# Masks in two float32r parts, a place of its own for one tile's values, and the head's order: one edit to an attention and expert kernel

## The chip, the cores and the metric

One Trainium2 chip, one core. The metric is the device time of one execution in microseconds (us); three executions of the kernel before gave 692.93, 693.51 and 694.43, so the median is 693.51.

## The reference

The reference is an attention followed by a gated feed-forward layer. For 4 batches of 8 heads, 768 positions and 64 dimensions, each query sees the keys within 15 positions of its own, and besides them 24 summary keys, one for each block of 32 positions (the maximum of the block's keys, with log 32 added to their scores). The softmax runs over both together, and the values are the positions' own and the blocks' means:

```python
k_sum = k.reshape(B, H, nb, block, D).max(axis=3)
v_sum = v.reshape(B, H, nb, block, D).mean(axis=3)
scores_l_m = np.where(mask_l, scores_l, -1000000000.0)
scores_all = np.concatenate([scores_l_m, scores_s], axis=-1)
...
return np.matmul(a, v_all).astype(np.float32)
```

Its result, 3072 rows of 512, goes through `(x @ w_a * (x @ w_b)) @ w_out` with 1536 hidden columns.

## The kernel before

**Units.** A tile is 128 query rows, and a unit (`u`) is two tiles, so 24 tiles make 12 units. The hidden columns are cut into 12 slices `f` of 128. The pair (unit, slice) is an item: `hidden` (L977) makes 24 float32r matmuls of 256 columns for both products, ScalarE and VectorE multiply them and split the result in two parts (`gh`, `gl`), and `down` (L996) adds six float32r matmuls of 512 columns into two banks. The 144 items are nearly all of TensorE's work. Their order is (0,0), (0,1), (1,0), (0,2), (1,1), (0,3) and so on, then units 2 to 11 one after the other (L1023).

**Weights.** The weights reach the kernel as 64-bit numbers, in 36 parts of 512 KB (w_a, w_b and w_out of each slice), two parts to a pair `j` (0 to 17), so slice f uses parts 3f, 3f+1 and 3f+2. `convert(j)` (L290) turns a pair into two float32r parts: for each half a ScalarE pass (L313) and three VectorE passes (L321, L328, L334), then a ScalarE copy (`hi`, L366) and two GpSimd passes (L371, L377, the second writes `lo`). The last three run over the whole pair at once, or, where `single` holds, over one half at a time. For pairs 0 and 1 and the last four `single` holds.

**The first two units** (tiles 0 to 3, L768 to L883) have a softmax of their own: `masks` (L590) writes the mask into two banks by a float32 matmul against the identity, the scores (L604) are added to it, VectorE takes the maxima (L637), ScalarE the exponentials (L649), VectorE makes a diagonal of the reciprocal sums (L671), TensorE turns and scales by it (L692), ScalarE copies the result (L704), and `values` (L755, matmuls L737) multiplies with the tile's values. The result is split into `x` (L745, L748), and a unit's items need the `x` of both its tiles. `begin(g)` (L825) makes query turn, masks and scores of tile g, `end(g)` (L838) the rest. Values lie in `vbuf` for tiles 0 and 2 and in `vw1` for tiles 1 and 3, so the load for tile 2 waits for the product of tile 0. The block means of the values are made once (L848 to L871) and copied by GpSimd from `vbuf` to `vw1` (L874).

**Order.** Every operation is given to `work.add` with an engine, a rank, an estimated duration and the names it reads and writes; `emit` (L72) is a list scheduler that writes the program out, engine by engine, by estimated times. The table `ORDER` (L23) shifts, for the operation of a given number, its rank and gives it an estimated time before which it isn't placed. These times exist in the planning only; on the chip each engine runs its instructions in the order written. SP issues all loads in one queue. Unit 2's attention (`FILL`) is spread among the conversions; its tile's GpSimd passes are L679.

Of the kernel before, what the change touches and what calls it, by code (L numbers as in the profile page):

```python
# [20 lines left out]


ORDER = {  # L23
# [15 lines left out]
}  # L39


# [65 lines left out]
def attention_moe(  # L107
# [10 lines left out]
    nc = tc.nc  # L118
# [96 lines left out]


    spaces = {n: sb([P, 2048], n) for n in ("S0", "S1")}
    for j in (*range(8, 13), *range(NW - 3, NW)):
        spaces[f"W{j}"] = wp.tile([P, 2048], F32, tag=f"W{j}", name=f"space{j}")

    pown = spaces["S0"][:, 2 * CV :].rearrange("p (h c x) -> p h c x", h=2, x=P)
# [5 lines left out]
    def spot(i):  # L227
        n, x = f"W{8 + i // 2}", i % 2 * 2
        return spaces[n][:, x * 512 : (x + 2) * 512], (f"{n}.{x}", f"{n}.{x + 1}")


    work = Work({"POOL": 10.0, "DVE": 4.0, "ACT": 3.0, "PE": 4.0, "SP": 0.8})
# [57 lines left out]
    def convert(j):  # L290
        rank = CONVERT + j / 6
        rk = [f"raw{2 * j}", f"raw{2 * j + 1}"]

        if j < NW - 4:
            space = {12: "W16", 13: "W17"}.get(j, ("W17", "W16", "W15", "S0")[j % 4])
            places = [(space, 0, 2), (space, 1, 3)]
            single = j < 2
        else:
            places = [slots[(2 * (j - NW + 4) + h) % 3] for h in range(2)]
            places = [(n, x, x + 1) for n, x in places]  # L300
            single = True
        cols = [[slice(x * CV, (x + 1) * CV) for x in xs] for _, *xs in places]
        fx, px = [[spaces[places[h][0]][:, cols[h][x]] for h in range(2)] for x in range(2)]
        fk, pk = [[f"{places[h][0]}.{places[h][1 + x]}" for h in range(2)] for x in range(2)]
        spans = [(h,) for h in range(2)] if single else [(0, 1)]

        def scale(h):
            high = raws[j][:, 2 * h * CV : 2 * (h + 1) * CV].rearrange("p (n t) -> p n t", t=2)
            nc.scalar.activation(  # L313
                bank["c0"], high[:, :, 1].bitcast(F32), AF.Prelu, scale=2.0**-112, alpha=-(2.0**32)
            )


        def step(n, h):
            f, p, e, s = fx[h], px[h], bank["c0"], bank["c1"]
            if n == 0:  # L320
                nc.vector.tensor_scalar(  # L321
                    out=f.bitcast(I32), in0=e.bitcast(I32), scalar1=3, scalar2=None,
                    op0=ALU.logical_shift_left,
                )
            elif n == 1:


                nc.vector.tensor_scalar(  # L328
                    out=s.bitcast(I32), in0=f.bitcast(I32), scalar1=-(1 << 23), scalar2=None,
                    op0=ALU.bitwise_and,  # L330
                )
            else:
                low = raws[j].rearrange("p (n t) -> p n t", t=2)[:, h * CV : (h + 1) * CV, 0]
                nc.vector.scalar_tensor_tensor(  # L334
                    out=p, in0=low.bitcast(U32), scalar=2.0**-52, in1=s, op0=ALU.mult, op1=ALU.mult
                )

        for n, h in [(n, h) for h in range(2) for n in range(3)]:
            f, p, e, s, r = [fk[h]], [pk[h]], ["c0"], ["c1"], [rk[h]]
            if n == 0:  # L340
                act(CHAIN, 0.52, r, e, lambda h=h: scale(h))
            reads, writes = ((e, f), (f, s), (r + s, p + [f"done{j}"] + r))[n]
            dve(rank, 0.6, reads, writes, lambda n=n, h=h: step(n, h))

        def parted(part):
            if j not in homes:
                homes[j] = wp.tile([P, 8, 2, P], F32R, tag=f"W{j}", name=f"w{j}")
            return homes[j][:, :, part, :]

        for hs in spans:  # L350
            ms = slice(4 * hs[0], 4 * (hs[-1] + 1))
            f, p, hi, lo = (
                [x[h] for h in hs] for x in (
                    fk, pk, [f"hi{2 * j}", f"hi{2 * j + 1}"], [f"lo{2 * j}", f"lo{2 * j + 1}"]
                )
            )
            x0 = spaces[places[hs[0]][0]]
            f8, p8 = (
                x0[:, cols[hs[0]][x].start : cols[hs[-1]][x].stop].rearrange(
                    "p (m n) -> p m n", n=P  # L360
                )
                for x in range(2)
            )
            act(
                rank - 0.5, 0.25 + 0.37 * len(hs), f + rk, hi,
                lambda ms=ms, f8=f8: nc.scalar.copy(out=parted(0)[:, ms], in_=f8),  # L366
            )
            takes = 0.2 + 1.1 * len(hs)
            pool(
                rank + 0.1 * hs[0], takes, hi, f,  # L370
                lambda ms=ms, f8=f8: nc.gpsimd.tensor_tensor(  # L371
                    out=f8, in0=f8, in1=parted(0)[:, ms].bitcast(F32), op=ALU.subtract
                ),
            )
            pool(
                rank + 0.1 * hs[0], takes, f + p, lo,
                lambda ms=ms, f8=f8, p8=p8: nc.gpsimd.tensor_tensor(  # L377
                    out=parted(1)[:, ms], in0=f8, in1=p8, op=ALU.add
                ),
            )  # L380
# [201 lines left out]
    def scores(u, t, qT, qk, s, sk, banks, diag=None, lead=None):  # L582
# [6 lines left out]

        def masks():  # L590
            for h in range(2):
                nc.tensor.matmul(
                    bank[banks[h]].rearrange("p (c x) -> p c x", x=P), ident,
                    mask[:, kind, None, :].broadcast_to([P, NP, P]), start=True, stop=False,
                )

        def fn():
            for c in range(NP):
# [10 lines left out]
                        )  # L609

        if masked:
            pe(rank + 0.1, 1.8, [], banks, masks)
        if lead is None:
            pe(-1, 1.2, [qk] + KT, banks, fn)
        else:
# [151 lines left out]

    def first_attention():  # L768
        first_keys()
        q0, qk = spot(3)  # L770
        for t in range(2):
            load(
# [25 lines left out]
        k0, k1 = key  # L798
        vk1 = [k0, k1, k1 + "b", k0 + "s", k1 + "s"]

        vin = []
        for i in range(6):
            x, key = spot(4 + i // 2)
# [4 lines left out]
            vin.append((x, key))  # L808
        load_values(0, 0, vbuf, VK[:3], 16)
        load_values(0, 1, vw1, vk1[:3], 18)  # L810

        q1, qk1 = spot(1)
        for t in range(2):
# [24 lines left out]
        def end(g, bk):  # L838
            u, i = g // G, g % G
            transposes(u, g, s[i], sk[i], [f"o{2 * i}", f"o{2 * i + 1}"], pts[i])  # L840
            values(u, g, (vbuf, vw1)[i], (VK, vk1)[i], bk, pts[i])

        for t in range(2):
            begin(t, f"h{t}")
# [19 lines left out]
        for e, r0 in ((0, WIN), (1, 32)):  # L864
            rows = slice(r0, r0 + 32)
            act(
                FIRST, 0.6, ["h0"], [VK[3 + e]],
                lambda e=e, rows=rows: nc.scalar.copy(
                    out=vbuf[e][rows].rearrange("p h d -> p (h d)"), in_=bank["h0"][rows]
                ),  # L870
            )  # L871
            pool(
                FIRST, 0.8, [VK[3 + e]], [vk1[3 + e]],
                lambda e=e, rows=rows: nc.gpsimd.tensor_copy(out=vw1[e][rows], in_=vbuf[e][rows]),  # L874
            )
        end(0, "h1")
        load_values(0, 2, vbuf, VK[:3], 20.5)
        begin(2, "o0")
        end(1, "h0")
        load_values(0, 3, vw1, vk1[:3], 20.7)  # L880
        begin(3, "o2")
        end(2, "o0")
        end(3, "o2")  # L883
# [196 lines left out]
```

## Time and profile before

| | us |
|---|---|
| median of three executions | 693.51 |
| the profiled execution | 693.23 |
| its span from the first to the last instruction | 691.5 |
| TensorE busy in the span | 676.8 |
| VectorE, ScalarE, GpSimd busy | 433.4, 252.7, 186.2 |

The profiled execution is 1.73 us longer than its span (start and end of the program), and 0.28 us below the median. The profile names the engines PE (TensorE), PEld (its weight load), ACT (ScalarE), DVE (VectorE), POOL (GpSimd) and SP (SyncE, here the queue of the loads). A float32 matmul shows as two records, a float32r one as one. An idle time in brackets says what ended it.

### The profile page before, as it was taken

Reading aid. Unit: us, or ns where it says so; the run is one execution under the profiler, and the core shown is the slowest. Engines: PE = TensorE matmul, PEld = TensorE weight load, DVE = VectorE, ACT = ScalarE, POOL = GpSimd, SP = SyncE. Lnnn points to the kernel's source line nnn. Section 1 sums busy time; section 2 is a strip of 40 time slices with the busy share of each in tenths; the row PEclk is TensorE's granted clock in tenths of the full one; section 3 lists DMA queues with packets and bytes.
Section 4 is the critical chain, followed back from the end, with each engine's and each line's share of the span. In section 5 each row is a group of like instructions: output and inputs, shape, how many; then the busy total and the mean of one; then the engine's idle time right before and its main releaser. Section 6 shows DMA issues by size and latency. Waiting matters only on the chain.

```text
span 691.5 us, 15093 instructions
## 1 busy us (share of the span) xinstructions
PE 676.8 (98%) x5988; PEld 621.5 (90%) x5988; DVE 433.4 (63%) x988; ACT 252.7 (37%) x795; POOL 186.2 (27%) x226
## 2 busy tenths in 40 slices
PE   6799999999999999999999999999999999999997
PEld 4589999998999999999999999999999999999996
DVE  3899999986676668766764767653662762212221
ACT  4886565523323333134333232332332332211211
POOL 5669899732433210412110110110110110000000
PEclk9999999999999999999999999999999999999999
DMA  9999863465144126431212311300200100000000
GB/s 229 260 276 225 267 163 121 81 134 111 49 103 104 40 40 124 96 72 42 53 24 60 67 29 46 67 1 22 66 22 2 54 22 1 31 1 1 32 1 31
DMA packets 154943, 54.84 MB, mean 79 GB/s; under 512 B 132456, under 2 KB 147816, under 8 KB 154872
## 3 DMA queue, kind: packets, MB, share of 16 engines
q1 hardware_dynamic: 154872, 53.88, 33.4%
q8 instruction: 47, 0.77, 0.5%
q14 instruction: 24, 0.20, 0.1%
HBM read 47.12 MB, written 6.29 MB: 77 GB/s over the span
## 4 chain that ended last, share of the span: by engine, by line
PE 93%; DMA 2%; SPq 2%; DVE 1%; ACT 1%; issue 0%; POOL 0%; ACTq 0%
PE h L965 57%; PE o L1001 29%; PE o L737 2%; PE c L737 2%; SPq L249 2%; PE c L604 2%; PE o L604 1%; DMA raw<-in_moe_w_out_dram 1%; DMA space<-in_v_dram 1%; PE o L692 1%; SPq L278 0%; DVE nml L637 0%; ACT s L649 0%; DVE pt L671 0%; ACT c L313 0%
## 5 line engine op out<-in xcount | busy, mean ns | idle before, releaser
L965 PEld LDWEIGHTS h<-x,w 128*128 128x128 f32 x3456 | 413.1, 188 | 10.5 <-issue 0.2
L965 PE MATMUL h<-x,w 128*128 128x256 f32 x3456 | 415.4, 277 | 0.0
L985 DVE TENSOR_TENSOR h<-h,g 128x256 f32<-128x256 f32 x144 | 62.0, 431 | 165.2 <-ACT g L982 163.4
L1001 PE MATMUL o<-w,gh 128*128 128x512 f32 x576 | 157.6, 396 | 0.0
L982 ACT COPY g<-h 128x256 f32<-128x256 f32 x144 | 53.6, 372 | 282.3 <-PE h L965 281.5
L1001 PEld LDWEIGHTS o<-w,gh 128*128 128x128 f32 x576 | 99.0, 188 | 17.2 <-ACT x L745 1.5
L679 POOL TENSOR_TENSOR s<-s,nml 128x512 f32<-128x512 f32 x40 | 41.6, 1041 | 242.6 <-DVE nml L664 242.1
L723 DVE STREAM_TRANSPOSE pt<-s 32x256 f32<-32x256 f32 x228 | 99.4, 436 | 5.6 <-POOL s L679 1.5
L1001 PE MATMUL o<-w,gl 128*128 128x512 f32 x288 | 90.2, 394 | 0.0
L990 DVE TENSOR_TENSOR gl<-h,gh 128x256 fp32r<-128x256 f32 x144 | 60.6, 421 | 30.9 <-ACT gh L987 29.4
L649 ACT ACTIVATE s<-s,nml 128x128 f32<-128x128 f32 x160 | 62.3, 392 | 43.9 <-DVE nml L637 43.9
L987 ACT CAST gh<-h 128x256 fp32r<-128x256 f32 x144 | 53.4, 371 | 60.7 <-DVE h L985 60.2
L1001 PEld LDWEIGHTS o<-w,gl 128*128 128x128 f32 x288 | 53.7, 188 | 11.8 <-issue 0.3
L534 POOL TENSOR_TENSOR S<-S 96x64 f32<-96x64 f32 (+3 forms) x54 | 35.5, 657 | 40.5 <-DMA S<-in_v_dram 29.5
L649 ACT ACTIVATION_READ_ACCUMULATOR s<-s,nml 128x1 f32 x160 | 30.1, 188 | 0.0
L371 POOL TENSOR_TENSOR space<-space,w 128x1024 f32<-128x1024 f32 (+1 forms) x13 | 26.8, 2063 | 6.0 <-ACT w L366 5.8
L658 DVE TENSOR_SCALAR nml<-nml 128x4 f32<-128x4 f32 x40 | 9.5, 239 | 28.6 <-ACT s L649 28.6
L313 ACT ACTIVATE c<-raw 128x512 f32<-128x512 f32 x36 | 23.3, 647 | 11.2 <-DVE space L321 4.1
L377 POOL TENSOR_TENSOR w<-space 128x1024 fp32r<-128x1024 f32 (+1 forms) x13 | 26.8, 2059 | 1.0
L637 DVE TENSOR_REDUCE nml<-s 128x4 f32<-128x512 f32 x40 | 25.3, 666 | 0.0
L433 POOL COPY kT<-ksum 128x144 f32<-128x144 f32 x16 | 4.7, 306 | 66.7 <-DVE ksum L511 52.0
L371 POOL TENSOR_TENSOR S<-S,w 128x512 f32<-128x512 f32 (+1 forms) x11 | 17.5, 1595 | 6.8 <-ACT w L366 6.8
(104 smaller groups left out, 457.3 us busy)
## 6 DMA issues: line engine op xcount, KB each, us to landing
raw<-in_moe_w_a_dram SPq DMA_DIRECT2D x12, 512.0 KB
raw<-in_moe_w_b_dram SPq DMA_DIRECT2D x12, 512.0 KB
raw<-in_moe_w_out_dram SPq DMA_DIRECT2D x12, 512.0 KB
out_dram<-S SPq DMA_DIRECT2D x24, 256.0 KB
qin<-in_q_dram SPq DMA_DIRECT2D x160, 32.0 KB
S<-in_v_dram SPq DMA_DIRECT2D x24, 192.0 KB
vw<-in_v_dram SPq DMA_DIRECT2D x18, 192.0 KB
kin<-in_k_dram SPq DMA_DIRECT2D x24, 100.0 KB
```

What stands on the lines that cost most here:

```text
L371: lambda ms=ms, f8=f8: nc.gpsimd.tensor_tensor(out=f8, in0=f8, in1=parted(0)[:, ms].bitcast(F32), op=ALU.subtract),
L534: lambda: nc.gpsimd.tensor_tensor(out=out, in0=i0, in1=i1, op=ALU.add),
L649: lambda h=h, c=c, sums=sums: nc.scalar.activation(s[h][:, c, :], x[h][:, c, :], AF.Exp, bias=m[:, 0, h, c : c + 1], scale=1.0, accum_out= ...
L679: lambda h=h, r=r: nc.gpsimd.tensor_tensor(out=s[h], in0=s[h], in1=r[:, :, None].broadcast_to([P, NP, P]), op=ALU.mult,),
L723: lambda js=js, qs=qs: nc.vector.transpose(out=pv[js, :, qs], in_=sv[qs, :, js]),
L737: nc.tensor.matmul(ps[h * D : (h + 1) * D, c, es], vw[e][:, 2 * c + h, :], d[:, h, c, es], start=True, stop=True, tile_position=(0, h * D),)
L965: nc.tensor.matmul(ps, w[:, c, part, :], x[xpart][:, c, :], start=(i == 0), stop=(i == n - 1))
L982: act(CHAIN, 0.38, [hk], [gk], lambda: nc.scalar.copy(out=g, in_=pa))
L985: lambda: nc.vector.tensor_tensor(out=pa, in0=pb, in1=g, op=ALU.mult),
L987: act(CHAIN, 0.41, [hk], [ghk], lambda: nc.scalar.copy(out=gh, in_=pa))
L990: lambda: nc.vector.tensor_tensor(out=gl, in0=pa, in1=gh.bitcast(F32), op=ALU.subtract),
L1001: nc.tensor.matmul(bank[ok[j]], (gh if first else gl)[:, js], w[:, :, part, :], start=(f == 0 and first and part == 0), stop=(f == NF - 1 ...
```

## The change

Four edits. (1) GpSimd makes a float32r copy of the identity and of two of the three masks, as a rounded part and a remainder, and `masks` adds both parts with float32r matmuls (estimate 0.96 in place of 1.8). (2) Tile 2's values get a place `vw2`, are loaded with those of tiles 0 and 1, and GpSimd copies the block means there too; tile 3 loads into `vbuf`. (3) `convert` takes the pair j = 2 half by half. (4) The table `ORDER` is replaced by another; as operations come and go, the numbers stand for others than before. Cut to its core:

```diff
-    136: (0, 41.8), 139: (38.79, 0), 141: (-0.3, 32.8), 142: (-3.38, 36.5), 149: (7.63, 29.8),
...
+    54: (31.73, 15.8), 55: (-2.09, 15.8), 56: (1.09, 14.9), 69: (30, 20.8), 76: (3.37, 22.1),
...
+    141: (-0.15, 41), 143: (19.54, 37.9), 144: (29.29, 0), 147: (-7.99, 32.8), 148: (0, 34.2),
...
+    235: (0, 46.4), 236: (-69.66, 47.4), 240: (47.6, 14), 241: (6.98, 14), 242: (-5.91, 42.5),
...
+    356: (1.15, 79.1), 405: (-40.68, 88.5), 412: (29.12, 89.5), 420: (19.57, 0),
...
-    for j in (*range(8, 13), *range(NW - 3, NW)):
+    for j in (*range(8, 14), *range(NW - 3, NW)):
...
+    x, MK = spot(10)
+    x = x.bitcast(F32R)
+    identr = x[:, :P]
+    maskr = [
+        x[:, n : n + 2 * P].rearrange("p (i x) -> p i x", x=P) for n in (P, 4 * P)
+    ]
...
-            single = j < 2
+            single = j < 3
...
-                nc.tensor.matmul(
-                    bank[banks[h]].rearrange("p (c x) -> p c x", x=P), ident,
-                    mask[:, kind, None, :].broadcast_to([P, NP, P]), start=True, stop=False,
-                )
+                for part in range(2):
+                    nc.tensor.matmul(
+                        bank[banks[h]].rearrange("p (c x) -> p c x", x=P), identr,
+                        maskr[part][:, kind, None, :].broadcast_to([P, NP, P]),
+                        start=(part == 0), stop=False,
+                    )
...
-            pe(rank + 0.1, 1.8, [], banks, masks)
+            pe(rank + 0.1, 0.96, MK, banks, masks)
...
+        for takes, fn in (
+            (0.3, lambda: nc.gpsimd.tensor_copy(out=identr, in_=ident)),
+            (0.45, lambda: nc.gpsimd.tensor_copy(out=maskr[0], in_=mask[:, :2, :])),
+            (0.6, lambda: nc.gpsimd.tensor_tensor(
+                out=maskr[1], in0=mask[:, :2, :], in1=maskr[0].bitcast(F32), op=ALU.subtract
+            )),
+        ):
+            pool(-1, takes, [], MK, fn)
...
+        x, (k0, k1) = spot(2)
+        vw2 = [x[:, e * 512 : (e + 1) * 512].rearrange("p (h d) -> p h d", d=D) for e in range(2)]
+        vk2 = [k0, k1, k1 + "b", k0 + "s", k1 + "s"]
+        work.add("-", 0, 0, 0, (), vk2, lambda: None)
...
+        load_values(0, 2, vw2, vk2[:3], 18.5)
...
-            values(u, g, (vbuf, vw1)[i], (VK, vk1)[i], bk, pts[i])
+            values(u, g, (vbuf, vw1, vw2, vbuf)[g], (VK, vk1, vk2, VK)[g], bk, pts[i])
...
+            for dst, dk in ((vw1, vk1), (vw2, vk2)):
...
-        load_values(0, 2, vbuf, VK[:3], 20.5)
...
-        load_values(0, 3, vw1, vk1[:3], 20.7)
+        load_values(0, 3, vbuf, VK[:3], 20.7)
```

## Rows read from the trace of the kernel before

**Rows 1.** The page: TensorE's total; VectorE's busy tenths in 40 slices of 17.3 us

```profile
PE 676.8 (98%) x5988; PEld 621.5 (90%) x5988; DVE 433.4 (63%) x988; ACT 252.7 (37%) x795; POOL 186.2 (27%) x226
...
DVE  3899999986676668766764767653662762212221
```

**Rows 2.** Chain that ended last, 0 to 140 us: start, duration, what

```profile
24.75 8.94 DMA raw<-in_moe_w_out_dram
...
33.77 0.64 ACT c L313
...
45.94 2.92 PE h L965 x24
...
72.77 1.37 PE o L1001 x6
```

**Rows 3.** TensorE in order of time, 0 to 120 us: start, duration, instructions

```profile
30.06 1.98 PE L592 MATMUL o<-mask,ident 128*128 128x512 f32 x4 [0.32 <-ACT qT L832]
...
34.97 1.98 PE L592 MATMUL o<-mask,ident 128*128 128x512 f32 x4 [1.45 <-ACT space L832]
36.88 1.15 PE L737 MATMUL h<-space,space 128*64 128x64 f32 x32
...
39.97 3.00 PE L965 MATMUL h<-x,w 128*128 128x256 f32 x24
...
44.79 1.15 PE L737 MATMUL o<-pt,vw 128*64 128x64 f32 x30 [0.59 <-ACT pt L704]
45.87 2.99 PE L965 MATMUL h<-x,w 128*128 128x256 f32 x24
...
54.59 5.61 PE L965 MATMUL h<-x,w 128*128 128x256 f32 x48
...
63.03 5.62 PE L965 MATMUL h<-x,w 128*128 128x256 f32 x48
...
99.93 2.91 PE L965 MATMUL h<-x,w 128*128 128x256 f32 x24
```

**Rows 4.** ScalarE and SP in order of time, around 34 us

```profile
34.34 0.58 ACT L832 ACTIVATE space<-o 128x512 f32<-128x512 f32 x1
...
34.18 3.65 SPq L249 DMA_DIRECT2D vw<-in_v_dram  x3
```

**Rows 5.** Mask matmuls (L592) by stretch: length, PE and PEld busy, granted clock, DMA share, GB/s

```profile
5.20:8.60 3.40, 3.33 (x4) 1.08 (x4) 1.00 1.31 223
...
12.00:14.00 2.00, 1.86 (x4) 0.55 (x4) 1.00 1.08 347
```

**Rows 6.** All engines by stretch: length, PE, PEld, DVE, ACT, POOL busy, clock, DMA, GB/s

```profile
20.00:30.00 10.00, 7.85 (x75) 6.33 (x74) 8.37 (x18) 9.61 (x34) 4.39 (x7) 1.00 1.17 264
30.00:40.00 10.00, 8.49 (x117) 5.59 (x117) 8.88 (x18) 8.38 (x27) 8.70 (x7) 1.00 1.15 292
```

**Rows 7.** GpSimd in order of time, 27 to 100 us

```profile
27.19 1.27 POOL L874 COPY space<-vw 32x512 f32<-32x512 f32 x2 [4.37 <-ACT vw L868]
28.55 1.28 POOL L371 TENSOR_TENSOR space<-space,w 128x512 f32<-128x512 f32 x1
...
43.15 2.36 POOL L377 TENSOR_TENSOR w<-space 128x1024 fp32r<-128x1024 f32 x1
49.31 2.38 POOL L371 TENSOR_TENSOR S<-S,w 128x1024 f32<-128x1024 f32 x1 [3.80 <-ACT w L366]
51.77 2.40 POOL L377 TENSOR_TENSOR w<-S 128x1024 fp32r<-128x1024 f32 x1
54.82 2.43 POOL L371 TENSOR_TENSOR space<-space,w 128x1024 f32<-128x1024 f32 x1 [0.65 <-ACT w L366]
...
62.34 2.42 POOL L377 TENSOR_TENSOR w<-space 128x1024 fp32r<-128x1024 f32 x1
...
92.33 1.04 POOL L679 TENSOR_TENSOR s<-s,nml 128x512 f32<-128x512 f32 x1
...
97.24 2.42 POOL L377 TENSOR_TENSOR w<-S 128x1024 fp32r<-128x1024 f32 x1
```

More of the change, by code (lines that the diff above doesn't have):

```diff
@@ L229, in spot @@
         return spaces[n][:, x * 512 : (x + 2) * 512], (f"{n}.{x}", f"{n}.{x + 1}")
+    x, MK = spot(10)
[4 more added lines that the diff above has]
+    ]
+    MK = list(MK)
     work = Work({"POOL": 10.0, "DVE": 4.0, "ACT": 3.0, "PE": 4.0, "SP": 0.8})
@@ L871, in first_attention @@
             )
[L872 to L875, printed above, removed]
+            for dst, dk in ((vw1, vk1), (vw2, vk2)):
+                pool(
+                    FIRST, 0.8, [VK[3 + e]], [dk[3 + e]],
+                    lambda e=e, rows=rows, dst=dst: nc.gpsimd.tensor_copy(
+                        out=dst[e][rows], in_=vbuf[e][rows]
+                    ),
+                )
         end(0, "h1")
-        load_values(0, 2, vbuf, VK[:3], 20.5)
         begin(2, "o0")
         end(1, "h0")
-        load_values(0, 3, vw1, vk1[:3], 20.7)
+        load_values(0, 3, vbuf, VK[:3], 20.7)
         begin(3, "o2")
```

28 rows, old and new, of the table ORDER are left out of this document.

## The prediction, made before the changed kernel was run

> **What bounds the kernel now.** I read the page first: TensorE is busy for 676.8 of 691.5 us [rows 1], so there are under 15 us in which it stands still, and a tuning of the head can win no more than a part of these plus whatever TensorE work it removes. Next the chain that ended last, from its early end: up to about 45 us it runs over loads, ScalarE and VectorE, and from 45.94 us on over TensorE alone [rows 2]. So the time is the moment at which TensorE starts to run without gaps, plus a fixed amount of matmul work behind it. Then TensorE's own order of time [rows 3]: the first item starts at 39.97, the second at 45.87, and between 30 and 46 us it idles three times: 0.32 us, 1.45 us and 0.59 us. The long one, ahead of 34.97, is tile 3's mask waiting for its query turn to be read by ScalarE (34.34 to 34.92 [rows 4]), and that reading stands in ScalarE's queue behind a conversion that waited for weights landing at 33.69 [rows 2]. Tile 1's product, ready to run, is behind that mask and starts at 36.88; on it hangs the `x` of unit 0 and so the first item.
>
> What could hold TensorE back after that is the supply of weights. VectorE is at nine tenths or more from the second to the eighth slice [rows 1], and it idles only 1.63 + 1.12 = 2.75 us between 20 and 40 us [rows 6]. GpSimd writes the last part of a pair, and how late that is shows the slack: pair 3 ends at 51.77 + 2.40 = 54.17, item (0,2) starts at 54.59; pair 5 ends at 64.76, item (0,3), the second half of the block at 63.03, starts at 65.8; pair 11 ends at 99.66, item (0,7) starts at 99.93 [rows 3, 7]. The slack is 0.4, 1.0 and 0.3 us. A gain in the head stays a gain only if these three move too.
>
> **The change part by part.**
>
> Masks. A tile's masks are two float32 matmuls in four records: 1.91 us from 34.97 to the next start at 36.88 [rows 3]. Six float32r matmuls of the same 512 columns take 1.37 us in steady flow [rows 2], 0.23 each, so the four new ones take 0.92. That is 1.0 us less for each of four tiles. Tiles 0 and 1 stand in a stretch where TensorE waits for loads, so I count nothing there: the cover is the loads, and without it each would give its 1.0. Tiles 2 and 3 stand at 30.06 and 34.97 on the path to the first items, and I count 0.95 each, 1.9 together.
>
> GpSimd's three preparing passes (a 128x128 copy, a 128x256 copy, a 128x256 subtraction) have no row of their own; from below they cost nothing beside the loads, from above one two-input 128x512 pass each (1.28 us [rows 7]), 3.8 us. They stand before the first score, in a stretch in which GpSimd has only the mask's making behind it. I take nothing on the path. The two more copies of the block means are 0.64 us each like the two at 27.19, 1.3 us; these start after a wait of 4.37 us [rows 7], and if they are late they push pair 0 behind them by 1.3. Pairs 0 to 2 can bear that: with it and ten half passes of 1.3 each behind 28.55, pair 2's first half is ready at 42.9, before the second item's place. So I take nothing and keep 1.3 for the range.
>
> Tile 2's values. The load moves from 34.18 [rows 4] to the loads of tiles 0 and 1. It was not the wait: tile 2's product at 44.79 waited for ScalarE's copy of the turned scores [rows 3]. By itself this part is worth nothing. It costs three issues in SP's queue and (96 + 32 + 64) rows of 2 KB, 384 KB, at 264 GB/s [rows 6] 1.5 us, ahead of weights that land at 33.69. Those are pair 2's second half, whose copy the new table holds to 47.4 planned us, so the cover is that later use; if it is gone, the pair is 1.5 us late. Tile 3's load into `vbuf` waits for tile 0's product as tile 2's did.
>
> Pair 2 by halves. Item (0,1) needs the first half only (part 4). Before, both halves end together at 43.15 + 2.36 = 45.51 [rows 7], just ahead of the item at 45.87 [rows 3], so without this part nothing won earlier could start the second item earlier. Two half passes of 1.28 us let the first half be ready about 2.5 us sooner; the price is 4 x 1.28 = 5.1 us for 4.8.
>
> The order. Counting the operations through, the new table places tile 1's product (now 148) from 34.2 planned us, before from 36.5, and no longer behind tile 3's masks. I therefore count the 1.45 us of TensorE's wait as won. It holds the first half of pair 2 to 46.4 and the second to 47.4, which says that they go behind other work in their queues; the first query turn of unit 2 goes to 79.1 planned us, so its softmax passes, two of 1.04 us at 92.33 ahead of pair 11 [rows 7], go later.
>
> The sum. 1.9 + 1.45 = 3.35 us are won before the second item. How much of it lasts is set by supply: at (0,7) 0.3 of slack plus the 2.1 of the two passes that move behind pair 11, 2.4; at (0,3) 1.0 plus the 2.75 that VectorE idles early, 3.75. The smallest is 2.4 us. The profiled execution's 693.23 becomes 690.8; the median stands 0.28 above it, so I forecast 691.1. Bounds: below, all three waits between 30 and 46 us (2.36) and both masks (1.9) are won and supply refuses nothing, 4.3 us, so 689.2, and a part of tile 0's and 1's masks may come on top; above, nothing is won and the 1.3 of the copies reaches the path, 694.8.
>
> **The rivals.**
>
> The supply binds at once. VectorE has no work less than before, and the conversions decide at 54.17, 64.76 and 99.66 [rows 7]. If its new order brings pairs 3 to 5 no earlier, TensorE only waits later, and the gain is the slack, 0.3 us: 693.2. For it: the holds of pairs 3 and 8 in the new table lie within a microsecond or two of the old planned places. Against it: (1,0) can run before (0,2) once unit 1 is ready, which gives pair 3 another 2.75 us.
>
> The clock. The four records of tile 0's mask take 3.33 us of busy time in 5.2 to 8.6 us and another tile's 1.86 in 12 to 14 [rows 5], so TensorE ran there at about half rate (the lower of 1.2 and 2.4 GHz), though the row's granted clock reads 1.00, and full rate came after this dense work. Now the masks wait for GpSimd, and the early stretch holds only turns between loads. If the low rate lasts until the masks of tiles 0 and 1 are done, these cost 2 x 0.92 more, 1.8 us, and the gain shrinks to 0.6: 692.9. The Trainium skill, "TensorE: Matmul & The Clock Gate", section "What's actually happening", says that the throttled state is the default and that activity releases it; by that rule, taking dense early work out speaks against this change. That the rate doubled behind the masks agrees with it; no row shows what fewer columns would do.
>
> Slower: GpSimd's queue. It idles 3.80 us before pair 3's first pass at 49.31, then only 0.65 before pair 4 [rows 7]. Pair 2's second half, 2.6 us, fits into the 3.80 if its ScalarE copy ends by 46.7. If the copy, held back in the plan, comes after that and still stands ahead of pair 3, pairs 3 to 5 come up to 2.0 us later (2.6 less 0.65). Item (0,3), with 1.0 of slack, is then 1.0 late, and `down` of (0,2), whose weights from pair 4 end at 54.82 + 2 x 2.43 + 0.1 = 59.8 and which follows the block at 54.59 at 60.1, 1.7 late; taken without any of the gain, 693.5 + 1.6 = 695.1. The point that decides is the end of that copy, before or after 46.7.
>
> More than forecast. If unit 1's items, run before (0,2), cover every supply gap, the 4.3 us of the lower bound come: 689.2.
>
> **How the numbers follow.** About 0.2% (1.4 us) is what a measurement of this kernel tells from no change. The forecast of 691.1 has 0.45 and more than it 0.14, together 0.59 for faster. The supply (0.16) and the clock (0.09) give 0.25 for no change. The queue of GpSimd has 0.16 for slower. The waits on the path are seen in rows and the new order goes around the longest, which is why the forecast leads; that supply has three tight places is why it has no more. The range of 688.6 to 694.8 takes in the forecast, the two cases of no change, the case of more with a little over it, and the milder part of the slower one, and leaves out some 0.2, most of it above.
>
> **What would show it.** Right: mask records in float32r, 0.9 us a tile; tile 1's product ahead of tile 3's mask, before 35 us; the first item by 37.5 us and the second before 44; no TensorE idle of over 0.5 us behind it, and item (0,7) some 2.4 us earlier than 99.93. Wrong: TensorE idle before (0,2), (0,3) or (0,7) with GpSimd named as the releaser (supply, or the queue if pair 3's first pass comes after 49.31), turns of keys at half rate past 9 us (clock), or scores of tile 0 waiting for GpSimd's mask parts.

## The result, and the profile after

The changed kernel takes 694.45 us (median of 20 executions, 693.92 to 695.40), the kernel before beside it 693.52: ratio 1.0012, interval 1.0006 to 1.0017. It is 0.9 us slower. The profiled execution has a span of 692.9 us, before 691.5.

The page of the kernel after, totals, against [rows 1]:

```profile
PE 677.9 (98%) x5988; PEld 624.5 (90%) x5988; DVE 434.4 (63%) x988; ACT 252.2 (36%) x796; POOL 188.9 (27%) x233
```

TensorE is busy 1.1 us longer although the masks shrank. TensorE of the kernel after, in order of time (start, duration, instructions), against [rows 3]:

```profile
30.05 1.20 PE L605 MATMUL o<-space 128*128 128x512 f32 x4
...
33.22 0.73 PE L605 MATMUL o<-space 128*128 128x512 f32 x2 [0.27 <-ACT space L718]
33.95 1.16 PE L751 MATMUL h<-space,space 128*64 128x64 f32 x32
...
37.82 3.10 PE L995 MATMUL h<-x,w 128*128 128x256 f32 x24 [1.68 <-DVE x L762]
...
46.42 2.98 PE L995 MATMUL h<-x,w 128*128 128x256 f32 x24
...
51.92 2.91 PE L995 MATMUL h<-x,w 128*128 128x256 f32 x24
...
68.68 2.99 PE L995 MATMUL h<-x,w 128*128 128x256 f32 x24
...
79.65 5.82 PE L995 MATMUL h<-x,w 128*128 128x256 f32 x48
...
94.40 3.01 PE L995 MATMUL h<-x,w 128*128 128x256 f32 x24 [0.49 <-DVE gl L1020]
...
100.78 1.20 PE L1031 MATMUL o<-w,gh 128*128 128x512 f32 x4 [0.62 <-ACT gh L1017]
...
109.32 2.99 PE L995 MATMUL h<-x,w 128*128 128x256 f32 x24
```

The same view of the kernel before, at the places with the same work done:

```profile
69.86 2.91 PE L965 MATMUL h<-x,w 128*128 128x256 f32 x24
...
80.74 5.62 PE L965 MATMUL h<-x,w 128*128 128x256 f32 x48
...
108.17 2.91 PE L965 MATMUL h<-x,w 128*128 128x256 f32 x24
```

The first item starts 2.15 us earlier (37.82, before 39.97), the second 0.55 later (46.42, before 45.87). A lead is read where both have done the same: the seventh item (six items, five `gh` and five `gl` groups done) starts at 68.68 and at 69.86, so the head has won 1.18 us. Nine items on, at 109.32 and 108.17, the change is 1.15 behind: 2.33 us are lost in 40 us. The two bracketed waits are 1.11 of it. Most of the remaining 1.2 is pitch, the time from the start of one matmul to the start of the next: the block of 48 matmuls takes 5.82 us, before 5.62, at a granted clock of 1.00 in both, and over these nine items a matmul takes 117.0 ns on average, before 114.3, which is 0.6 us.

The waits come from VectorE. Start and duration on VectorE of the kernel after, the softmax sums of unit 2:

```profile
89.50 2.37 DVE L672 TENSOR_SCALAR nml<-nml 128x4 f32<-128x4 f32 x1
91.90 0.18 DVE L678 RECIPROCAL nml<-nml 128x4 f32<-128x4 f32 x1
92.00 0.41 DVE L1015 TENSOR_TENSOR h<-h,g 128x256 f32<-128x256 f32 x1
92.31 0.91 DVE L672 TENSOR_SCALAR nml<-nml 128x4 f32<-128x4 f32 x1
```

GpSimd of the same kernel at that time, and below it GpSimd and VectorE of the kernel before:

```profile
89.45 2.40 POOL L389 TENSOR_TENSOR w<-space 128x1024 fp32r<-128x1024 f32 x1
92.16 1.04 POOL L693 TENSOR_TENSOR s<-s,nml 128x512 f32<-128x512 f32 x1 [0.32 <-DVE nml L678]
```

```profile
87.45 2.42 POOL L371 TENSOR_TENSOR space<-space,w 128x1024 f32<-128x1024 f32 x1 [1.70 <-ACT w L366]
...
89.31 0.60 DVE L658 TENSOR_SCALAR nml<-nml 128x4 f32<-128x4 f32 x1
...
92.58 0.81 DVE L658 TENSOR_SCALAR nml<-nml 128x4 f32<-128x4 f32 x1
```

An addition of 1e-9 to 512 numbers takes 2.37 us where it begins just behind a GpSimd pass of 2.40, and both end within 0.02 us; the next takes 0.91 beside a pass of 1.04. Before, the first began late in such a pass (87.45 + 2.42) and took 0.60. The item's product (L1015) stands behind the addition, and the waits at 94.40 and 100.78 behind that. The Trainium skill, "SBUF — State Buffer", section "Who interferes with whom", says that a `tensor_scalar`, which this addition is, can take the pair of ports that VectorE shares with GpSimd, and that whoever issues first then holds it for its whole instruction while the other is blocked; these rows agree.

### The profile page after: what moved, and what is told of

Read it like the earlier page. It is cut to its first block, busy times and chain, and to the rows that moved or that the text cites. A ratio compares the mean times of both kernels' runs of the same rounds, so it can differ in the third digit from the quotient of the medians.

```text
span 692.9 us, 15107 instructions
## 1 busy us (share of the span) xinstructions
PE 677.9 (98%) x5988; PEld 624.5 (90%) x5988; DVE 434.4 (63%) x988; ACT 252.2 (36%) x796; POOL 188.9 (27%) x233
## 4 chain that ended last, share of the span: by engine, by line
PE 92%; DVE 3%; ACT 3%; issue 1%; DMA 1%; SPq 0%; ACTq 0%
PE h L995 55%; PE o L1031 29%; PE o L751 2%; PE c L751 2%; PE c L618 2%; PE o L618 2%; ACT s L663 1%; ACT space L663 1%; DMA space<-in_k_dram 1%; DVE c L340 1%; DVE nml L672 0%; DVE space L346 0%; ACT c L325 0%; PE o L410 0%; PE o L706 0%
## 5 line engine op out<-in xcount | busy, mean ns | idle before, releaser
L1015 DVE TENSOR_TENSOR h<-h,g 128x256 f32<-128x256 f32 x144 | 62.0, 430 | 165.6 <-ACT g L1012 164.0
L672 DVE TENSOR_SCALAR nml<-nml 128x4 f32<-128x4 f32 x40 | 11.3, 285 | 28.6 <-ACT s L663 28.6
```

The source lines that it names most:

```text
L1015: lambda: nc.vector.tensor_tensor(out=pa, in0=pb, in1=g, op=ALU.mult),
```

## The experiments

Every ratio is against the kernel before on the same chip, with its 95% interval.

**The addition.** Leave it out for units 2 to 11 (each sum holds exp(0) = 1, so in float32 it changes nothing).

```diff
-                lambda r=r: nc.vector.tensor_scalar(
+                lambda r=r: None if not masked else nc.vector.tensor_scalar(
```

> The changed kernel without the addition of 1e-9 to the softmax sums of units 2 to 11 (a 128x4 VectorE instruction from and to SBUF; the sums are at least 1, so in float32 the addition changes nothing). Its place in the plan is kept, so the order is the same. In the changed kernel one such instruction takes 2.37 us at 89.50, as long as a GpSimd pass of 2.40 that began at 89.45, and another 0.91; TensorE then idles 0.49 at 94.40 and 0.62 at 100.78. Theory C (VectorE is held up by GpSimd there, and that stall makes TensorE's two waits): the waits go, 1.1 us less than the changed kernel, about 693.3. Theory D (the two waits come from the order in which conversions and items stand on VectorE, late anyhow): 0.3 us or less.

Measured: 693.42 us, 0.9996 [0.9987, 1.0005], 1.03 below the changed kernel; both waits are gone.

> The kernel before without the 1e-9 added to the softmax sums of units 2 to 11. In its trace the two additions of unit 2 that stand beside GpSimd's conversions took 0.60 and 0.81 us in place of 0.16, and TensorE did not wait for them. Theory 'the lock on the addition is what the change runs into, and the kernel before does not': no gain here, 693.2 to 693.7, and the changed kernel without the addition (693.42) is then 0 to 0.3 us away from it. Theory 'the addition costs both kernels the same': 1.0 us faster, 692.5.

Measured: 693.25 us, 0.9994 [0.9984, 1.0003], 0.5 below the kernel before beside it, with an interval that takes in no change. The addition costs the change about 1.0 us; what it costs the kernel before is 0.5 by the medians, and by the interval anything from nothing to 1.1. Without it the two kernels are level (0.9996 and 0.9994).

Is it the instruction's form or just one more instruction? A reciprocal of the same sums into a place that nothing reads took the addition's place:

```diff
+    spare = sb([P, NP], "spare")
...
+                lambda r=r: nc.vector.reciprocal(out=spare, in_=r) if not masked
+                else nc.vector.tensor_scalar(
```

> The changed kernel with the 1e-9 addition of units 2 to 11 replaced by a reciprocal of the same 128x4 sums into a spare place that nothing reads: as many VectorE instructions, of the same size, in the same places. Theory 'it is the form of the instruction' (a one-input addition from SBUF to SBUF waits until GpSimd's pass is done, a reciprocal does not, its rows are 0.18 everywhere): the instruction takes 0.18 beside GpSimd's passes, the waits ahead of 94.40 and 100.78 are gone and the time is as without it, 693.4. Theory 'any VectorE instruction in that place is late' (queue, ScalarE's sums): the 2.37 us and the two waits stay, 694.4.

Measured: 708.33 us, 1.0211 [1.0197, 1.0225], and neither theory had that. The reciprocals took 0.17 and the two waits were gone, yet nearly every matmul of the items was slower. The small `spare` had moved the tiles allocated behind it, all weights among them, by 32 bytes. So once more with 256 bytes:

> As e2_recip (the 1e-9 addition of units 2 to 11 replaced by a reciprocal of the same size into a spare place), but the spare place takes 256 bytes of a partition in place of 16, so that the weights behind it lie at the same remainder by 256 bytes as in the changed kernel. Theory 'e2_recip was slow by its weights' place, not by its instruction': TensorE's pitch in the items is 113 to 118 ns as in the changed kernel, the reciprocals take 0.18, the waits ahead of 94.40 and 100.78 are gone, and the time is that without the addition, 693.2 to 693.7. Theory 'the reciprocal costs it': 708 again.

Measured: 693.25 us, 0.9991 [0.9982, 1.0]. GpSimd and VectorE of this run where the first addition stood:

```profile
89.55 2.40 POOL L390 TENSOR_TENSOR w<-space 128x1024 fp32r<-128x1024 f32 x1
...
89.61 0.17 DVE L673 RECIPROCAL spare<-nml 128x4 f32<-128x4 f32 x1
89.81 0.18 DVE L680 RECIPROCAL nml<-nml 128x4 f32<-128x4 f32 x1
```

As many instructions, of the same size, in the same place and again just behind the start of a GpSimd pass, and 1.2 us less: it is the form.

**The masks.** Float32 masks again, the order kept:

```diff
-                for part in range(2):
-                    nc.tensor.matmul(
-                        bank[banks[h]].rearrange("p (c x) -> p c x", x=P), identr,
-                        maskr[part][:, kind, None, :].broadcast_to([P, NP, P]),
-                        start=(part == 0), stop=False,
-                    )
+                nc.tensor.matmul(
+                    bank[banks[h]].rearrange("p (c x) -> p c x", x=P), ident,
+                    mask[:, kind, None, :].broadcast_to([P, NP, P]), start=True, stop=False,
+                )
```

> The changed kernel with masks made by float32 matmuls again, as before (two matmuls in four records a tile), everything else and the written order kept. Theory 'the masks' time is worth what the prediction took' (0.95 for each of tiles 2 and 3 on the path, 1.9 us): the first item starts at 39.7 in place of 37.82 and the time is 694.45 + 1.9 = 696.3. Theory 'covered': the first item waits 1.68 us for the VectorE pass that writes x, and that pass is queued behind conversion passes of VectorE, so the masks of tiles 2 and 3 may grow by 0.95 each with the first item moved by under 0.5; the next items wait for GpSimd's weights anyway: 694.2 to 695.0.

Measured: 694.50 us, 1.0012 [1.0004, 1.0021], as the changed kernel. TensorE of this run:

```profile
33.55 1.98 PE L604 MATMUL o<-mask,ident 128*128 128x512 f32 x4
...
38.24 3.10 PE L993 MATMUL h<-x,w 128*128 128x256 f32 x24 [0.59 <-DVE x L760]
```

The longer masks ate the wait ahead of the first item (1.68 became 0.59) and moved it by 0.42. Covered.

**Pair 2.** The copy `hi` of a half writes the weights over the raw tile of the whole pair, so it waits until VectorE has read both halves. Here the halves have tiles of their own, and the entries 231, 235 and 236 of the table are gone, so the run takes both together:

```diff
+            if j == 2:
+                raws[j, i % 2] = wp.tile([P, 1024], I32, tag=f"W{j}{i % 2}", name=f"raw{i}")
+                dst = raws[j, i % 2]
...
-                rank - 0.5, 0.25 + 0.37 * len(hs), f + rk, hi,
+                rank - 0.5, 0.25 + 0.37 * len(hs), f + ([rk[hs[0]]] if j == 2 else rk), hi,
```

> The changed kernel with pair 2's two halves in places of their own, so that the copy of the first half no longer waits for the second half's VectorE passes, and with the holds and shifts of operations 231, 235 and 236 taken out of the table. Theory 'the second item's weights were the gate, as the prediction took it': the second item starts at about 43.5 in place of 46.42 and the end comes 1 to 2.5 us earlier, 692 to 693.4. Theory 'supply behind it decides': the second item starts near 43.5, but (1,0) waits for the x of unit 1 and (0,2) for pair 3, whose passes come no earlier than VectorE lets them; TensorE idles in front of those instead, and the time stays within 0.5 of 694.45.

Measured: 695.45 us, 1.0025 [1.0012, 1.0038]. TensorE of this run:

```profile
42.88 3.07 PE L1071 MATMUL h<-x,w 128*128 128x256 f32 x24
...
49.34 1.20 PE L1107 MATMUL o<-w,gh 128*128 128x512 f32 x4 [0.32 <-DVE x L838]
...
52.31 0.38 PE L1071 MATMUL h<-x,w 128*128 128x256 f32 x1
53.18 2.90 PE L1071 MATMUL h<-x,w 128*128 128x256 f32 x23 [0.49 <-DVE x L838]
```

The second item starts 3.5 us earlier and the time is 1.0 longer. It pushes tiles 2 and 3 back on TensorE; (1,0) needs their `x` and gets it 1.1 later (53.18 less the matmul already done, against 51.92). The second theory had the gate right and the cost too low.

**The clock.** Two float32 matmuls of the identity ahead of the first key turn:

```diff
+    for _ in range(2):
+        nc.tensor.matmul(
+            bank["o3"].rearrange("p (c x) -> p c x", x=P), ident,
+            ident[:, None, :].broadcast_to([P, NP, P]), start=True, stop=True,
+        )
```

> The changed kernel with two extra float32 matmuls of 512 columns, of the identity with itself into a bank not yet used, ahead of the first turn of keys (3.4 us of work at the lower clock in a stretch in which TensorE waits for the first load; what they write is overwritten). Theory E (the head is late because the clock rises later than before: the turns of keys take 1.1 us each up to 11 us and the first mask 1.86 us): the clock rises by about 8 us, masks of tile 0 take 0.92, the scores of tile 0 start about 1 us earlier than 14.88, and 0.5 to 1.0 us less than the changed kernel in all, 693.4 to 693.9. Theory F (early time is covered by later waits on ScalarE and VectorE): within 0.2 us of the changed kernel although the masks are faster.

Measured: 694.52 us, 1.001 [1.0001, 1.0019]. TensorE of this run, and a stretch of it (length, PE, PEld, DVE, ACT, POOL busy, granted clock, DMA, GB/s):

```profile
7.98 0.63 PE L410 MATMUL c<-ident,space 128*128 128x128 f32 x4 [0.55 <-DMA space<-in_k_dram]
9.18 0.63 PE L410 MATMUL c<-ident,space 128*128 128x128 f32 x4 [0.56 <-DMA space<-in_k_dram]
10.30 1.12 PE L410 MATMUL o<-ident,space 128*128 128x128 f32 x4 [0.50 <-DMA space<-in_k_dram]
```

```profile
10.30:13.60 3.30, 3.08 (x11) 2.49 (x12) 1.38 (x2) 1.44 (x4) 2.21 (x7) 0.50 1.22 269
```

A group of four turns takes 1.1 us in the changed kernel up to 12 us (half rate). Here the two at 7.98 and 9.18 take 0.63, each after a wait of 0.55 for its load, so up to 10 us the half rate costs nothing. But behind these waits the granted clock fell to 0.50 (the lower of the two levels) from 10.3 to 13.6 us, turns took 1.12 again, and the first item of this execution starts at 39.01, in the changed kernel at 37.82. So what the half rate behind 10 us costs is not shown by this run. A pair of profiles below speaks for a cost: e3_no_add_pad64 and e3_pad64 differ by the addition alone, which stands far behind the head; the first had a granted clock of 0.57 from 12 to 16 us and its first item at 37.52, the second 1.00 and 35.85.

**The pitch and the place of the weights.** First, is it the new tile (`W13` in the list of spaces) that moved most weights by 8 KB? The list's order puts them back in the change, or moves them in the kernel before:

```diff
-    for j in (*range(8, 14), *range(NW - 3, NW)):
+    for j in (*range(8, 13), *range(NW - 3, NW), *range(8), 13):
```

> The changed kernel with one thing undone: the added work space of weight pair 13 is reserved last, so that every other tile lies at the address that it had before the change (in the changed kernel the homes of weight pairs 0 to 7 and three scratch spaces lie 8 KB higher). Order, instructions and data are the changed kernel's. Theory A (where the tiles lie slows TensorE's pace: 24 matmuls of an item take 2.82 us from 55 to 131 us in the changed kernel, 2.75 before): the pace goes back to 2.75, 18 items at 0.10 us each, so 1.8 us less than the changed kernel, about 692.7. Theory B (the pace belongs to that execution or to the new order, not to the addresses): same as the changed kernel, 694.4, and a pace of 2.82 if it is the order's.

> The kernel before with one thing added: the work space of pair 13 is reserved where the changed kernel reserves it, and not used. Only addresses differ. Theory A (addresses slow TensorE's pace): 1.8 us slower than before, about 695.3, and 24 matmuls at 2.82 us between 55 and 131 us. Theory B (the pace is not the addresses'): same as before, 693.5, at 2.75.

Measured: 694.19 us, 1.0008 [0.9998, 1.0017], and 693.87, 0.9999 [0.9991, 1.0008]. Steps of 8 KB don't matter. Small steps do, as `e2_recip` had shown. Unused bytes went ahead of the weights' tiles, or ahead of `x`:

```diff
+    wp.tile([P, 8], F32, tag="pad", name="pad")
```

> The changed kernel with 32 unused bytes of a partition ahead of the weights' places, nothing else: all weights then lie at 32 by the remainder of 64 bytes, before at 0. Theory 'weights that don't begin at a multiple of 64 bytes slow every matmul of an item': the pitch is 115 to 122 ns nearly everywhere and the time 708, as in e2_recip. Theory 'the place does not matter': 694.45.

> The changed kernel with 64 unused bytes ahead of the weights' places: they then lie at 0 by the remainder of 128 and of 256 bytes, before at 64 and 192. Theory 'the pitch of 117.7 ns in some stretches comes from the weights' place, as at 32': it is 113.4 throughout and the time 1.3 to 4 us shorter (the excess over 113.4 is 1.7 before 140 us and 4.4 in all). Theory 'the stretches have another cause': the same stretches stay, 694.2 to 694.7.

> The changed kernel without the 1e-9 added to the softmax sums of units 2 to 11 and with 64 unused bytes ahead of the weights' places. Where the place of the weights sets the two values of the pitch: 689.5 to 692.2, faster than both kernels. Where it does not: as without the addition alone, 693.4.

> The changed kernel with 128 unused bytes ahead of the weights' places: they differ from x by 64 by the remainder of 128 as in the changed kernel, but by 192 in place of 64 by that of 256. Theory 'remainder of 128': 694.45, with the same stretches at 117.7 ns. Theory 'remainder of 256': slow, or without the stretches, 690 to 693.

> As e4_pad128 and without the 1e-9 added to the softmax sums of units 2 to 11. Where the weights' place leaves the stretches: 693.4, as without the addition alone; where it takes them away: 689.5 to 692.2.

> The changed kernel with x moved by 64 bytes of a partition and the weights by a multiple of 256 (64 unused bytes ahead of x, 192 behind it): x lies at 64 by the remainder of 128, as the weights do. Theory 'the place of the weights against that of x decides' (fast where they differ by 64 by the remainder of 128, slow where they differ by 0 or 96): slow, 708 to 711. Theory 'the place of the weights alone decides': 694.45.

> The changed kernel with 64 unused bytes ahead of x and no more, so that x, gh, gl and the weights all move by 64 bytes: their differences stay, the weights lie at 0 by the remainder of 128. Theory 'against x': 694.45. Theory 'the place of the weights alone': slow as e3_pad64, 710.

The places are those of the built programs (changed kernel: `x` from byte 31360, weights from 80320 in steps of 8192):

| kernel | place of weights less that of `x`, remainder by 256 | us | ratio |
|---|---|---|---|
| changed kernel | 64 | 694.45 | 1.0012 [1.0006, 1.0017] |
| e4_all64 | 64 | 692.76 | 0.9992 [0.9983, 1.0002] |
| e2_recip | 96 | 708.33 | 1.0211 [1.0197, 1.0225] |
| e3_pad32 | 96 | 709.44 | 1.0222 [1.0208, 1.0236] |
| e3_pad64 | 128 | 710.09 | 1.0235 [1.0219, 1.0252] |
| e3_no_add_pad64 | 128 | 710.62 | 1.0235 [1.0221, 1.0249] |
| e4_pad128 | 192 | 708.63 | 1.0222 [1.0206, 1.0237] |
| e4_no_add_pad128 | 192 | 707.15 | 1.0201 [1.0186, 1.0216] |
| e4_x64 | 0 | 712.02 | 1.027 [1.0254, 1.0285] |

It is the place against `x`, to 256 bytes: moving `x` alone is as bad as moving the weights alone, and moving both is good. The expectation that named a remainder by 64, and the one by 128, were wrong. TensorE of e4_pad128:

```profile
80.18 5.81 PE L996 MATMUL h<-x,w 128*128 128x256 f32 x48
...
102.83 5.82 PE L996 MATMUL h<-x,w 128*128 128x256 f32 x48
```

All of its blocks take what the changed kernel's block at 79.65 takes. From start to start a matmul takes 113 to 114 ns in the changed kernel from 74 to 76 us and from 94 to 98, 117 to 119 from 56 to 72, from 79 to 94 and from 102 to 129, and 117 to 119 nearly everywhere in e4_pad128. So the change runs for stretches at a pitch that another place makes the rule. What moves it from one to the other was not found: in the eight profiles with the order after and the difference of 64 the stretches agree from about 52 to 92 us and differ behind 100, and the excess over 113.4 ns, summed up to 140 us, is 1.1 to 1.8 us; in the four with the order before it is 0.35 to 0.82.

**What the head is bound by.** e4_all64 came out with its first item at 36.37. e3_pad64 had it early too (35.85), in spite of its slow items; e4_x64 and e4_pad128 did not (37.87, 37.99). What the first two share is that the weights' tiles, in which the early loads land too, begin at a multiple of 256 bytes, and that the loads ran faster from 4 to 35 us (289 and 297 GB/s, against 266 and 258). e3_no_add_pad64 shares the place as well; its clock, and its 37.52, are told above. The last two runs take this move and the missing addition together, in both kernels:

```diff
+    sb([P, 16], "pad0")
     xs = [[sb([P, NP, CH], f"x{i}_{p}", F32R) for p in range(2)] for i in range(2)]
```

> The changed kernel with 64 unused bytes ahead of x (all behind it moves by 64) and without the 1e-9 added to the softmax sums of units 2 to 11. Theory 'the two are independent': 692.8 less the 1.0 of the addition, 691.7, faster than both kernels by 0.2 to 0.4%. Theory 'e4_all64 won by chance or on that chip': 693.2 to 693.6, as without the addition alone.

> The kernel before with the same two edits. Theory 'the head's gain of the change is real, 1.2 us at 68 us, and it only met the addition and the pitch': 692.6 to 693.3, at least 0.9 above the run beside it. Theory 'the change is worth nothing by itself': within 0.4 of the run beside it.

Measured: the change 691.51 us, 0.9973 [0.9962, 0.9984]; the kernel before 691.61, 0.9969 [0.9955, 0.9983]. Both beat both kernels, by 2 to 3 us, and the change by itself is worth nothing that can be told (0.1 us). What the loads moved from 4 to 35 us, kernel before and then the kernel before with the two edits:

```profile
DMA packets 17562, 8.08 MB, mean 261 GB/s; under 512 B 11766, under 2 KB 17303, under 8 KB 17559
```

```profile
DMA packets 18500, 9.36 MB, mean 302 GB/s; under 512 B 11838, under 2 KB 18117, under 8 KB 18497
```

The kernel after, from 4 to 35 us, moves 264 GB/s, with the two edits 279. TensorE of the edited kernel before:

```profile
28.98 1.98 PE L593 MATMUL o<-mask,ident 128*128 128x512 f32 x4 [1.07 <-ACT qT L833]
...
32.80 1.98 PE L593 MATMUL o<-mask,ident 128*128 128x512 f32 x4 [0.36 <-ACT space L833]
...
44.10 3.01 PE L966 MATMUL h<-x,w 128*128 128x256 f32 x24
...
52.79 5.61 PE L966 MATMUL h<-x,w 128*128 128x256 f32 x48
...
68.26 2.99 PE L966 MATMUL h<-x,w 128*128 128x256 f32 x24
```

Nothing on TensorE's or VectorE's path to the first items was shortened there, and every place is 1.6 to 2.0 us earlier (39.97, 45.87 and 54.59 became 37.99, 44.10 and 52.79 [rows 3], and 69.86 became 68.26); the 1.45 us stall that the change was to go around is 0.36 by itself, and the 0.32 ahead of tile 2's mask 1.07. VectorE's, ScalarE's and GpSimd's instructions take as long as before from 4 to 45 us (means within 3%); what got faster is the loads. So the loads' rate sets most of the head's length. With the two edits the changed kernel's seventh item starts at 67.76 against 68.26, a lead of 0.50 in place of 1.18, and the pitch (5.82 against 5.62) has eaten it by 107 us (106.84 against 106.75). The Trainium skill, "DMA: Bandwidth & Descriptors", section "How a descriptor splits into AXI transactions", says that the first transaction of a descriptor that does not start at a multiple of 256 bytes starts at the multiple below it, which costs extra beats; it speaks of reads, and here the places that are written moved, so the rate of these loads agrees with it in direction only.

The clock took part of that lead. TensorE and a stretch of the changed kernel with the two edits:

```profile
36.41 4.49 PE L996 MATMUL h<-x,w 128*128 128x256 f32 x24 [2.14 <-DVE x L763]
```

```profile
36.40:40.70 4.30, 4.29 (x24) 4.29 (x25) 3.85 (x10) 4.07 (x21) 1.12 (x1) 0.63 1.16 313
```

TensorE idled 2.14 us, and the first item then ran at a granted clock of 0.63 on average (0.50 from 37 to 39 us) and took 4.49 us, without the edits 3.10. TensorE does not wait from there to the second item, so up to 1.4 us of the lead went there. The same shows in e4_all64 (4.61 us); in e3_pad64, after an idle of 2.15 us, the clock stayed at 1.00. In five of the eight executions of the change with the two edits the mean granted clock was 1.00; their median is 691.31, 0.3 below that of the kernel before with the same edits.

## Why the prediction was wrong

The forecast of 691.1 counted 3.35 us won before the second item and 2.4 kept; the lead was 1.18 us at the seventh item and had turned into a lag of 1.15 nine items on. Three steps of the sum failed: the masks' time was counted on the path, the second item's weights were taken for its gate, and nothing was set down for what the new order does behind the head, where a VectorE addition now meets a GpSimd pass (1.0 us). That 694.45 lies below the upper bound of 694.8 is luck: that bound adds 1.3 us for the copies of the block means, and what came was the addition and the pitch.

**Masks, 1.9 us: wrong.** The records are shorter, nearly as forecast (1.20 us for four where 1.98 stood [rows 3]; 1.13 from 30.05 to the next start, forecast 0.92), but on the path they are worth 0 to 0.4, as e2_masks_f32 shows. I took tiles 2 and 3 to be on it because tile 1's product, on which the first item hangs, stood behind tile 3's masks. The cover was VectorE: TensorE now waits 1.68 us for the pass that writes `x`.

**The stall, 1.45 us: half right.** It shrank from 1.45 [rows 3] to 0.27, but not because tile 1's product goes ahead: that still stands behind tile 3's masks (33.95 behind 33.22). I misread the table; what came earlier is the turn of tile 3's query (29.57, before 31.88). The first item came 2.15 us earlier, not 3.35. Which part of the new order brought that is not shown: no run took the order or `vw2` out alone.

**Pair 2 by halves, 2.5 us sooner: wrong.** I read the list of passes, not what the copy waits for. ScalarE of the kernel after, and GpSimd:

```profile
42.51 0.62 ACT L378 CAST w<-space 128x512 fp32r<-128x512 f32 x1
...
46.56 0.62 ACT L378 CAST w<-space 128x512 fp32r<-128x512 f32 x1
```

```profile
43.21 1.28 POOL L383 TENSOR_TENSOR space<-space,w 128x512 f32<-128x512 f32 x1 [4.21 <-DMA vw<-in_v_dram]
44.56 1.29 POOL L389 TENSOR_TENSOR w<-space 128x512 fp32r<-128x512 f32 x1
...
50.54 2.43 POOL L383 TENSOR_TENSOR S<-S,w 128x1024 f32<-128x1024 f32 x1 [0.61 <-ACT w L378]
```

The first half is ready at 44.56 + 1.29 = 45.85, no sooner than the whole pair was (45.51). GpSimd's idle 4.21 is put down to a load, but the pass that follows reads the copy of 42.51. And with the halves really apart the time grew: the second item was never the gate, unit 1's `x` was.

**Tile 2's values, "covered": wrong.** The second half of pair 2 was to be used late, but the first half waits for it. Its load is issued at 28.55, before at 24.75 [rows 2]:

```profile
28.55 1.12 SPq L290 DMA_DIRECT2D raw<-in_moe_w_out_dram  x1
```

**Supply.** I named VectorE and GpSimd as what could hold TensorE back. Whether the three tight places would have refused a larger gain was not tried; what sets most of the time up to 35 us is the loads' rate, which stood in the profile at 264 GB/s [rows 6] and which I used only to price a load. A head bound by loads gives little for TensorE work taken out of it.

**The slower side.** I gave it 0.16, by GpSimd's queue. Its condition came true (the second half's copy ends at 46.56 + 0.62 = 47.18, past 46.7) and pair 3's first pass moved from 49.31 [rows 7] to 50.54 above; but the lead of 1.18 us at 68.68 shows that the price, 1.6 us and all of the gain, was not paid there. The step that failed is that unit 2's softmax passes would go behind pair 11: they stayed (92.16, before 92.33 [rows 7]), while the addition ahead of them moved to the start of a GpSimd pass. I counted what GpSimd's passes do to each other and not what one does to a VectorE instruction. This is 1.0 us, shown by e1_no_add and e3_recip. The pitch, most of the other 1.2 us lost in the profiled pair, had no term in the sum: [rows 3] have 5.61 for a block of 48, and I took that for fixed. Why it changes stays open.

**The clock, early masks and block means.** The half rate is in the rows (turns of 1.1 us up to 12 us); up to 10 us it is worth nothing, as e1_warm shows, and what it costs behind that is open. GpSimd's preparing passes and copies are not seen on the path.

## What to carry to other kernels

Before counting what a shorter operation wins in a kernel's first stage, ask whether the loads' rate sets that stage: if TensorE's waits end with a DMA or with an engine that waited for one, the work taken out only makes a wait longer. A VectorE addition of 128x4 numbers between places in SBUF took as long as the GpSimd pass beside it (2.37 us), so look for short instructions with one long outlier, and move them, change their form or drop them. Compare matmul pitch in steady stretches of two kernels before explaining a difference by waits, and keep the places of the operands fixed, to the byte, when adding even a small tile.

## What the hardware showed beyond expectation

- The place of the stationary weights against the moving `x`: at a difference of 64 by the remainder of 256 bytes a matmul of 256 columns takes mostly 113 or 114 ns from start to start, at 0, 96, 128 and 192 it takes 115 to 124, and the kernel 14 to 18 us more. The Trainium skill, "SBUF — State Buffer", section "Who interferes with whom", gives TensorE two independent read ports and says that it never waits for another engine; in these runs its pitch depends all the same on where its two operands lie, and the measurement decides.
- Loads into places that begin at a multiple of 256 bytes ran at 302 GB/s in place of 261 from 4 to 35 us (in the change 279 in place of 264), which made the head 1.6 to 2.0 us shorter (0.9 to 1.4).
- Addition and reciprocal of the same 128x4 numbers, one-input operations both: just behind the start of a GpSimd pass of 2.40 us they take 2.37 us and 0.17 us.
- The granted clock fell to 0.50 in the middle of the head in four of the twenty profiles: from 10.3 to 13.6 us in e1_warm, for part of 12 to 16 us in e3_no_add_pad64, and in the first item of e4_all64 and of the changed kernel with the two edits, each time after TensorE had waited.
